# First stage of an attention and expert kernel: splits of queries and keys moved to GpSimd, a scaling moved to ScalarE, filler matmuls held in place

## The chip, the cores and the metric

The kernel runs on 1 core of one Trainium2 chip. The metric is device microseconds of one execution. Before the change three runs took 1026.7, 1026.74 and 1029.19 us, median 1026.74 us. The engines are TensorE (PE in the profile, with PEld for its weight loads), VectorE (DVE), ScalarE (ACT), GpSimd (POOL) and SyncE (SP), which issues nearly all DMAs.

## The reference

Inputs are q, k, v of shape (4, 8, 576, 64), that is 4 batches and 8 heads, a tau, and the weights of two further layers. Attention drops scores that lie more than tau below their row's maximum:

```
scores = scale * np.matmul(q, k.transpose(0, 1, 3, 2))
thresh = np.max(scores, axis=-1, keepdims=True) - tau
scores = np.where(scores >= thresh, scores, -1000000000.0)
attn = np.exp(scores - max);  attn = attn / (sum(attn) + 1e-09);  out = attn @ v
...
u = x + (x^T @ U @ V)^T ;  y = u + relu(u @ w_ch1) @ w_ch2          # channel layer
out[b, s] = p[e] * (relu(y[b, s] @ w1[e]) @ w2[e])                   # one expert of 8 per token
```

All is float32 at the borders. Operands of the large matmuls are split into a rounded high part and the rest (h and l in the names: kh, kl; w0h, w0l), so that two or three matmuls in a faster format give a product close to float32.

## The kernel before

Two heads form a pair, four pairs a batch. The first stage is the attention of batch 0 alone (attention_alone); after it each batch's attention runs interleaved with the channel layer of the batch before, then come routing and the experts.

In attention_alone a step handles one tile of 128 query rows of one head. There are 9 tiles in a pair (five groups, the last, g = 4, holds the 64 left-over rows of both heads in one tile), so 36 steps. A step's core: scores on TensorE into one of two PSUM banks (L320, L322), the row maximum on DVE (peak, L355), the limit on DVE (L359), the exponential on ScalarE (L366), threshold and row sum on DVE (mask, L370). Two steps later the result is transposed on TensorE (L423, L429) and copied out by ScalarE (L424), multiplied with v (L442 to L446), and a chain of small matmuls (L468 to L514) makes a slice of the channel layer's input.

Beside these steps runs what prepares later ones. load_pair brings a pair's keys and queries in four cuts (two of keys, two of queries) through three staging buffers called raw, which go round: each cut's DMA waits until the buffer's former user is done. Keys are rounded on ScalarE (L291) and their rest taken on GpSimd (L292); queries are scaled and rounded on ScalarE (L299), the rest on DVE (L301). A generator, conv, narrows 64-bit weights: a DMA brings a piece (cr, L203), ScalarE casts its upper part (top, L211), DVE joins the parts (w, L218), and a DMA writes the result to memory (wdram), from which load_w fetches it again (wr, L681) and splits it. For batch 0, load_w rounds the first two weight blocks on ScalarE (L688), later ones on GpSimd (L686).

Fillers are matmuls on constant data (idle, L592), issued by turn_over where a step has little TensorE work.

Each engine runs its instructions in one fixed order. A scheduler sets that order when the program is built, by its own model of time; an instruction marked with keep_in_program_order stays where it is written, and in this stage GpSimd's order is the written one. SP's queue is also in order: a DMA that waits for its buffer holds up every DMA behind it.

Of the kernel before, what the change touches and what calls it, by code (L numbers as in the profile page):

```python
# [14 lines left out]
AF = mybir.ActivationFunctionType  # L15
# [88 lines left out]
def attention_channel_moe(ctx, tc, qk, vv, tau, umat, vrep, wch, wgl, wexp, consts, out):  # L104
# [155 lines left out]
    def load_pair(b, hp, later=None):  # L260
# [9 lines left out]
            (1, 0, S), (1, S, QKW), (0, 0, 608), (0, 608, QKW))  # L270
        eng = dve if i == 0 or b > 1 else pool
        def steps():
            for n, (kq, c0, c1) in enumerate(cuts):
# [16 lines left out]
                if kq:  # L290
                    act.activation(kh[:, c], x, AF.Copy)  # L291
                    eng.tensor_tensor(out=kl[:, c], in0=x, in1=kh[:, c].bitcast(F32), op=ALU.subtract)  # L292
                elif i == 0 and c1 - c0 > 128:
                    lo, hi, xl = qs[64:128, c], qs[64:128, c].bitcast(F32), x[64:128]
# [30 lines left out]
    class Group:  # L325
# [47 lines left out]
        def norm(self):  # L373

            g = self.key[2]
            rv = self.rvs[:, g, 0:self.nh]
            if self.b >= SCALED:
                inverse(rv)
                for h in range(self.nh):
                    act.activation(self.pt[:, h], self.pt[:, h], AF.Copy, scale=rv[:, h:h + 1])  # L380
            elif g == 4:
                inverse(rv)
                sp.dma_start(out=self.rvs[:64, 4, 1:2], in_=self.rvs[64:, 4, 0:1])

# [69 lines left out]
    def chain(nm, hp, half, xT, xu, rvs):  # L454
# [20 lines left out]
        if half == 0:  # L475
            yield 0.3
            return
        if rvs is None:
            act.activation(xsd[:64, 4], tp[:64, 2], AF.Copy)
        else:  # L480
            for h in range(2):
                act.activation(xsd[:64, 4, h * 64:h * 64 + 64], tp[:64, 2, h * 64:h * 64 + 64], AF.Copy,
                               scale=rvs[:64, 4, h:h + 1])
        yield 0.3
# [75 lines left out]
    def attention_alone(b):  # L560
# [26 lines left out]
        def turn_over(n, nm):  # L587

            if n > 0:
                t = bank("tp", [128, 512], f"idle{nm}")  # L590
                for j in range(n):
                    x = pe.matmul(t, lhsT=idle[:, :128], rhs=idle, start=True, stop=True)  # L592
                    if j == 0 and nm in (0, 1, 2):
                        tc.keep_in_program_order(x)
# [3 lines left out]
        for i in range(len(seq) + 3):  # L598
# [21 lines left out]
            while pend and debt > 0:  # L620
                c = piece()
                debt -= c
                spent += c
            turn_over(int((0.8 - spent) / 0.2) + (4 if i == 0 else 0), i)
            if Q and qh == Q.nh - 1:
# [46 lines left out]
    def load_w(b, f):  # L672
# [6 lines left out]
        for i, bufs in ((0, W0), (1, W1)):  # L679
# [4 lines left out]
            eng = dve if b and (b < B - 1 or f < 8) else pool  # L684
            if b == 0 and f > 1:
                pool.tensor_copy(hi, x)  # L686
# [700 lines left out]
```

## Time and profile before

| | us |
|---|---|
| median of 3 runs | 1026.74 |
| the profiled execution | 1029.15 |
| its span, first to last instruction | 1027.4 |
| TensorE busy in the span | 993.8 (97%) |
| VectorE busy | 718.8 (70%) |
| ScalarE busy | 610.8 (59%) |
| GpSimd busy | 157.9 (15%) |

The profiled execution lies at the upper of the values that the timed runs show. A busy share is a mean over stages: the page's slices have TensorE at 8 or 9 tenths in the first five slices (to 128 us), at 9 or more after that to the end, while VectorE is at 6 to 9 tenths in the first half and 2 to 9 in the second. The first stage's last mask ends at 101.3 us, and the first matmul of the channel layer starts at 114.4 us. The mean TensorE clock over the span is 0.994.

### The profile page before, as it was taken

The page shows a single profiled execution, that of the slowest core. Times are in us where ns is not written, and L with a number is a line of the kernel's source. Part 1 is how long each engine was busy: PE and PEld are TensorE (multiplying, and loading weights), DVE is VectorE, ACT ScalarE, POOL GpSimd, SP SyncE. Part 2 cuts the span into 40 slices and gives each one's busy share as a digit, 9 for nine tenths or more (in the row PEclk, how much of TensorE's full clock was granted, in tenths as well). Part 3 has the DMA queues.
Part 4 walks back from the last instruction along what each step waited for, and adds up shares of the span by engine and source line. Part 5 has one row for each costly group of instructions (what it writes and reads, how often), then busy time and mean ns, then how long its engine had stood idle before and what let it go on. Part 6 is the DMA issues. An engine that isn't in the chain of part 4 may idle for free. (4 is left out here: it accounts for less than half of the span.)

```text
span 1027.4 us, 17797 instructions
## 1 busy us (share of the span) xinstructions
PE 993.8 (97%) x6309; PEld 831.8 (81%) x6309; DVE 718.8 (70%) x1771; ACT 610.8 (59%) x1242; POOL 157.9 (15%) x149
## 2 busy tenths in 40 slices
PE   8898899999999999999999999999999999999996
PEld 4666677778787787788888898999998798889884
DVE  7889787886778877877676564692469755566673
ACT  6787877776687777776565653432344344355562
POOL 3322145342000000000000000014400321120100
PEclk9999999999999999999999999999999999999998
DMA  7745487864323322423121110463154655566650
GB/s 216 240 126 168 144 265 241 281 204 150 114 97 92 123 80 77 125 95 89 56 68 42 42 45 28 140 212 127 39 196 151 201 178 185 174 193 198 194 184 16
DMA packets 58529, 143.72 MB, mean 140 GB/s; under 512 B 7421, under 2 KB 8573, under 8 KB 58432
## 3 DMA queue, kind: packets, MB, share of 16 engines
q1 hardware_dynamic: 55072, 132.27, 40.2%
q0 software_dynamic: 3360, 10.23, 3.0%
q8 instruction: 52, 0.85, 0.3%
q14 instruction: 45, 0.37, 0.1%
HBM read 124.65 MB, written 18.61 MB: 139 GB/s over the span
## 5 line engine op out<-in xcount | busy, mean ns | idle before, releaser
L1137 ACT ACTIVATE eh<-ew 128x512 fp32r<-128x512 f32 x160 | 94.0, 628 | 66.9 <-PE el L1253 51.8
L1138 DVE TENSOR_TENSOR el<-ew,eh 128x512 fp32r<-128x512 f32 x160 | 106.6, 692 | 37.4 <-ACT eh L1137 34.8
L370 DVE SCALAR_TENSOR_TENSOR p<-s,st,p 128x576 f32<-128x576 f32 x144 | 114.1, 814 | 18.5 <-ACT p L366 14.8
L710 PE MATMUL l<-uh,w0h 128*128 128x256 f32 (+2 forms) x352 | 126.7, 360 | 0.3 <-ACT yT L515 0.3
L366 ACT ACTIVATE p<-s,st 128x576 f32<-128x576 f32 x144 | 103.6, 739 | 34.9 <-DVE st L355 33.7
L711 PE MATMUL l<-ul,w0h 128*128 128x256 f32 (+2 forms) x352 | 122.6, 349 | 0.0
L712 PE MATMUL l<-uh,w0l 128*128 128x256 f32 (+2 forms) x352 | 122.3, 348 | 0.0
L355 DVE TENSOR_REDUCE st<-s 128x1 f32<-128x576 f32 x144 | 105.2, 749 | 16.2 <-PE s L322 15.2
L725 PE MATMUL l<-hh,w1h 128*128 128x512 f32 (+3 forms) x320 | 115.3, 360 | 0.0
L727 PE MATMUL l<-hh,w1l 128*128 128x512 f32 (+3 forms) x320 | 112.6, 352 | 0.0
L726 PE MATMUL l<-hl,w1h 128*128 128x512 f32 (+3 forms) x320 | 112.2, 351 | 0.0
L424 ACT ACTIVATE ptt<-tp 128x512 f32<-128x512 f32 (+1 forms) x192 | 88.6, 490 | 30.7 <-PE tp L423 30.5
L320 PE MATMUL s<-kh,qs 128*128 128x288 f32 x320 | 96.7, 321 | 7.1 <-DVE p L370 4.9
L689 POOL TENSOR_TENSOR w1l<-wr,w1h 128x512 fp32r<-128x512 f32 x24 | 32.4, 1359 | 457.9 <-DVE rha L995 426.2
L423 PE MATMUL tp<-cst,p 128*128 128x128 f32 x576 | 91.2, 276 | 2.6 <-ACT ptt L424 2.2
L730 DVE TENSOR_TENSOR yT<-l,yT 128x448 f32<-128x448 f32 (+2 forms) x96 | 50.0, 521 | 57.7 <-PE l L727 57.3
L322 PE MATMUL s<-kl,qs 128*128 128x288 f32 x320 | 89.6, 299 | 0.0
L380 ACT ACTIVATE p<-p,rv 128x576 f32<-128x576 f32 x108 | 78.6, 771 | 15.7 <-DVE rv L387 15.5
L423 PEld LDWEIGHTS tp<-cst,p 128*128 128x128 f32 x576 | 67.9, 140 | 19.2 <-ACT ptt L424 9.3
L320 PEld LDWEIGHTS s<-kh,qs 128*128 128x128 f32 x320 | 60.9, 190 | 17.1 <-DVE p L370 7.7
L443 PE MATMUL po<-ptt,v 128*64 128x256 f32 (+1 forms) x256 | 71.4, 416 | 2.2 <-ACT ptt L424 2.2
L442 PE MATMUL po<-ptt,v 128*64 128x256 f32 (+1 forms) x256 | 70.8, 416 | 1.3 <-ACT ptt L431 1.0
(610 smaller groups left out, 2441.1 us busy)
## 6 DMA issues: line engine op xcount, KB each, us to landing
ew<-in_wexp_dram SPq DMA_DIRECT2D x80, 512.0 KB, 4.5
wr<-wdram SPq DMA_DIRECT2D x128, 256.0 KB, 2.7
cr<-in_wch_dram SPq DMA_DIRECT2D x32, 512.0 KB, 5.4
raw<-in_qk_dram SPq DMA_DIRECT2D x30, 304.0 KB, 3.5
wdram<-w SPq DMA_DIRECT2D x32, 256.0 KB, 2.9
v<-in_vv_dram SPq DMA_DIRECT2D x16, 352.0 KB, 3.6
raw<-in_qk_dram SPq DMA_DIRECT2D x16, 320.0 KB, 3.1
raw<-in_qk_dram SPq DMA_DIRECT2D x16, 288.0 KB, 4.0
```

The lines of the kernel that those rows point to most:

```text
L320: pe.matmul(s["t"][:, h, :288], lhsT=qs[:, qc:qc + 128], rhs=kh[:, k0:k0 + 288], start=(j == 0), stop=False)
L355: dve.tensor_reduce(out=self.st[:, 0, h:h + 1], in_=self.t[h], axis=AX.XY, op=ALU.max, negate=True)
L366: act.activation(self.halves(h), self.t[h], AF.Exp, bias=self.st[:, 0, h:h + 1])
L370: dve.scalar_tensor_tensor(out=p, in0=self.t[h], scalar=self.st[:, 1, h:h + 1], in1=p, op0=ALU.is_ge, op1=ALU.mult, accum_out=self.rvs[:, ...
L423: pe.transpose(tp[:, c - c0], src[:, c * 128:c * 128 + 128], ident)
L710: pe.matmul(pm, lhsT=w1h[:, wk], rhs=uh[k], start=(k == 0), stop=False)
L711: pe.matmul(pm, lhsT=w1h[:, wk], rhs=ul[k], start=False, stop=False)
L712: pe.matmul(pm, lhsT=w1l[:, wk], rhs=uh[k], start=False, stop=(k == 3))
L725: pe.matmul(pm, lhsT=w2h[:, wd], rhs=xh, start=(f == f0), stop=False)
L726: pe.matmul(pm, lhsT=w2h[:, wd], rhs=xl, start=False, stop=False)
L727: pe.matmul(pm, lhsT=w2l[:, wd], rhs=xh, start=False, stop=(f == f0 + 3))
L1138: dve.tensor_tensor(out=lo, in0=x, in1=hi.bitcast(F32), op=ALU.subtract)
```

## The change

For pairs 1 to 4 (`own`; pair 4 is the first of batch 1) the rounding of keys moves from ScalarE to GpSimd, and the scaling, rounding and splitting of queries moves from ScalarE and DVE to three GpSimd instructions, a form used so far for two cuts of pair 0. The left-over tile of batch 0 is now normalised by ScalarE on the tile itself; before, its factors were moved to other partitions by a small DMA and applied later in two ScalarE copies. Fillers of every step but the first burst keep their place, and from step 4 on a step is filled to 1.5 units where it was 0.8. GpSimd rounds all of batch 0's weight blocks.

```
+        own = 1 <= i <= NPAIR
...
                 if kq:
-                    act.activation(kh[:, c], x, AF.Copy)
+                    if own:
+                        pool.tensor_copy(kh[:, c], x)
+                    else:
+                        act.activation(kh[:, c], x, AF.Copy)
                     eng.tensor_tensor(out=kl[:, c], in0=x, in1=kh[:, c].bitcast(F32), op=ALU.subtract)
-                elif i == 0 and c1 - c0 > 128:
+                elif own or i == 0 and c1 - c0 > 128:
                     lo, hi, xl = qs[64:128, c], qs[64:128, c].bitcast(F32), x[64:128]
                     pool.tensor_scalar(out=x, in0=x, scalar1=t8[:, 1:2], scalar2=None, op0=ALU.mult)
                     pool.tensor_copy(qs[:, c], x)
...
             elif g == 4:
                 inverse(rv)
-                sp.dma_start(out=self.rvs[:64, 4, 1:2], in_=self.rvs[64:, 4, 0:1])
+                act.activation(self.pt[:, 0], self.pt[:, 0], AF.Copy, scale=rv[:, 0:1])
...
-        if rvs is None:
-            act.activation(xsd[:64, 4], tp[:64, 2], AF.Copy)
-        else:
-            for h in range(2):
-                act.activation(xsd[:64, 4, h * 64:h * 64 + 64], tp[:64, 2, h * 64:h * 64 + 64], AF.Copy,
-                               scale=rvs[:64, 4, h:h + 1])
+        act.activation(xsd[:64, 4], tp[:64, 2], AF.Copy)
...
-                    if j == 0 and nm in (0, 1, 2):
+                    if j == 0 and nm != "a":
                         tc.keep_in_program_order(x)
...
-            turn_over(int((0.8 - spent) / 0.2) + (4 if i == 0 else 0), i)
+            turn_over(int(((1.5 if i > 3 else 0.8) - spent) / 0.2) + (4 if i == 0 else 0), i)
...
-            if b == 0 and f > 1:
+            if b == 0:
                 pool.tensor_copy(hi, x)
```

The program's order of instructions moves at three places. In the names, the first number is the pair (raw1_3: cut 3 of pair 1), in s, p, st and tp the numbers are batch, pair, group and head; the last number only tells buffers apart.

GpSimd's order from the end of pair 0's queries, before:

```order
L297 TENSOR_TENSOR qs0_97<-raw0_7_134,qs0_97 64x256
L292 TENSOR_TENSOR kl1_203<-raw1_0_204,kh1_202 128x576
L292 TENSOR_TENSOR kl1_203<-raw1_1_224,kh1_202 128x640
L236 TENSOR_TENSOR vst_65<-wv_0_342,vst_65 32x512 x2
L236 TENSOR_TENSOR vst_65<-wv_512_382,vst_65 32x64 x2
```

and now:

```order
L293 CAST kh1_202<-raw1_0_204 128x576
L296 TENSOR_TENSOR kl1_203<-raw1_0_204,kh1_202 128x576
L293 CAST kh1_202<-raw1_1_224 128x640
L296 TENSOR_TENSOR kl1_203<-raw1_1_224,kh1_202 128x640
L299 TENSOR_SCALAR raw1_2_242<-raw1_2_242,t8_63 128x608
L300 CAST qs1_201<-raw1_2_242 128x608
L301 TENSOR_TENSOR qs1_201<-raw1_2_242,qs1_201 64x608
L299 TENSOR_SCALAR raw1_3_279<-raw1_3_279,t8_63 128x608
L300 CAST qs1_201<-raw1_3_279 128x608
L301 TENSOR_TENSOR qs1_201<-raw1_3_279,qs1_201 64x608
L236 TENSOR_TENSOR vst_65<-wv_0_352,vst_65 32x512 x2
```

Two instructions on pair 1 have become ten; the last of them is the last reader of raw1_3. Pairs 2 to 4 read alike.

SP's queue has the same DMAs in the same order at that time in both programs; it stands now:

```order
L284 DMA raw1_3_279<-in_qk_dram 128x608
L308 DMA v1_200<-in_vv_dram 128x704
L203 DMA crv_512_323<-in_vrep_dram 128x256
L284 DMA raw2_0_478<-in_qk_dram 128x576
L284 DMA raw2_1_512<-in_qk_dram 128x640
L284 DMA raw2_2_541<-in_qk_dram 128x608
L203 DMA cr0_0_0_350<-in_wch_dram 128x2048
L203 DMA cr0_0_512_390<-in_wch_dram 128x2048
```

raw2_2 goes into the buffer of raw1_3, and cr0_0_0, the first piece of channel weights, is behind it. Where ScalarE turns from pair 0 to pair 1 (top is the cast of a piece, p0_1_0 the first exponential of pair 1), before:

```order
L291 ACTIVATE kh2_460<-raw2_0_462 128x576
L291 ACTIVATE kh2_460<-raw2_1_496 128x640
L366 ACTIVATE p0_0_4_322<-s0_0_4_0_324,st0_0_4_323 128x576
L449 ACTIVATE yT0_363<-po0_0_1_312 128x256
L424 ACTIVATE ptt0_0_2_365<-tp0_0_2_0_366 128x4x128
L211 ACTIVATE top1_88<-cr0_0_0_340 128x512
L424 ACTIVATE ptt0_0_2_365<-tp0_0_2_4_397 128x4x128
L424 ACTIVATE ptt0_0_2_365<-tp0_0_2_8_403 128x128
L211 ACTIVATE top0_87<-cr0_0_512_380 128x512
L366 ACTIVATE p0_1_0_349<-s0_1_0_0_352,st0_1_0_350 128x576
```

and now:

```order
L370 ACTIVATE p0_0_4_330<-s0_0_4_0_332,st0_0_4_331 128x576
L453 ACTIVATE yT0_373<-po0_0_1_320 128x256
L428 ACTIVATE ptt0_0_2_375<-tp0_0_2_0_376 128x4x128
L211 ACTIVATE top1_88<-cr0_0_0_350 128x512
L370 ACTIVATE p0_1_0_359<-s0_1_0_0_362,st0_1_0_360 128x576
L428 ACTIVATE ptt0_0_2_375<-tp0_0_2_4_407 128x4x128
L428 ACTIVATE ptt0_0_2_375<-tp0_0_2_8_413 128x128
L211 ACTIVATE top0_87<-cr0_0_512_390 128x512
L370 ACTIVATE p0_1_0_359<-s0_1_0_1_399,st0_1_0_360 128x576
L387 ACTIVATE p0_0_4_330<-p0_0_4_330,rv0_0_0_152 128x576
```

The two kh2 are gone, the cast of cr0_0_0 still stands ahead of the first exponential of pair 1, and the scaling of the left-over tile is new.

DVE's order in the third group of pair 1, before (TENSOR_REDUCE is peak, SCALAR_TENSOR_TENSOR on p is mask):

```order
L355 TENSOR_REDUCE st0_1_2_487<-s0_1_2_0_488 128x1
L355 TENSOR_REDUCE st0_1_2_487<-s0_1_2_1_514 128x1
L359 TENSOR_SCALAR st0_1_2_487<-st0_1_2_487,t8_63 128x1 x2
L386 TENSOR_SCALAR rv0_1_0_351<-rv0_1_0_351 128x4
L370 SCALAR_TENSOR_TENSOR p0_1_2_486,rv0_1_0_351<-s0_1_2_0_488,st0_1_2_487,p0_1_2_486 128x576
L370 SCALAR_TENSOR_TENSOR p0_1_2_486,rv0_1_0_351<-s0_1_2_1_514,st0_1_2_487,p0_1_2_486 128x576
```

and now:

```order
L359 TENSOR_REDUCE st0_1_2_503<-s0_1_2_0_504 128x1
L363 TENSOR_SCALAR st0_1_2_503<-st0_1_2_503,t8_63 128x1
L374 SCALAR_TENSOR_TENSOR p0_1_2_502,rv0_1_0_361<-s0_1_2_0_504,st0_1_2_503,p0_1_2_502 128x576
L476 TENSOR_TENSOR xsd0_0_1_382<-tx0_0_4_522,rv0_0_0_152 128x256
L359 TENSOR_REDUCE st0_1_2_503<-s0_1_2_1_533 128x1
L363 TENSOR_SCALAR st0_1_2_503<-st0_1_2_503,t8_63 128x1
L374 SCALAR_TENSOR_TENSOR p0_1_2_502,rv0_1_0_361<-s0_1_2_1_533,st0_1_2_503,p0_1_2_502 128x576
```

Peak and mask of one tile now follow each other, where two peaks came before two masks. On TensorE the program has 78 filler matmuls where it had 35.

## Rows read from the trace of the kernel before

**Rows 1.** Windows of three stretches: us, busy per engine (instructions), PEclk, DMA share, GB/s.

```profile
31.40:101.30 69.90, 60.47 (x433) 44.17 (x433) 61.75 (x147) 55.99 (x121) 19.15 (x15) 0.98 0.58 174
101.30:114.40 13.10, 10.81 (x78) 7.35 (x78) 10.64 (x27) 11.00 (x29) 0.00 (x0) 1.00 0.47 161
114.40:400.00 285.60, 281.90 (x1683) 218.49 (x1684) 219.26 (x483) 208.91 (x407) 60.08 (x58) 1.00 0.50 162
```

**Rows 2.** Timeline of GpSimd, 10 to 19 us: start, us, instruction, [idle before].

```profile
10.23 1.41 POOL L295 TENSOR_SCALAR raw<-raw,t 128x448 f32<-128x448 f32 x1 [8.06 <-DVE st L359]
11.71 0.56 POOL L296 CAST qs<-raw 128x448 fp32r<-128x448 f32 x1
12.36 1.13 POOL L297 TENSOR_TENSOR qs<-raw,qs 64x448 fp32r<-64x448 f32 x1
13.59 0.92 POOL L295 TENSOR_SCALAR raw<-raw,t 128x256 f32<-128x256 f32 x1
14.58 0.39 POOL L296 CAST qs<-raw 128x256 fp32r<-128x256 f32 x1
15.06 0.72 POOL L297 TENSOR_TENSOR qs<-raw,qs 64x256 fp32r<-64x256 f32 x1
15.86 2.93 POOL L292 TENSOR_TENSOR kl<-raw,kh 128x576 fp32r<-128x576 f32 x2
```

**Rows 3.** Timeline of DVE, SP and ACT, 22 to 32 us, some lines.

```profile
22.11 0.85 DVE L301 SCALAR_TENSOR_TENSOR qs<-raw,t,qs 64x608 fp32r<-64x608 f32 x1
...
22.99 0.33 SPq L283 DMA_DIRECT2D raw<-in_qk_dram  x1
23.47 0.33 SPq L203 DMA_DIRECT2D cr<-in_wch_dram  x1
...
28.86 0.79 ACT L211 ACTIVATE top<-cr 128x512 f16<-128x512 bf16 x1 [0.20 <-DMA cr<-in_wch_dram]
...
30.79 0.72 ACT L366 ACTIVATE p<-s,st 128x576 f32<-128x576 f32 x1
...
31.40 0.67 DVE L218 SCALAR_TENSOR_TENSOR w<-cr,top 128x512 int32<-128x512 int32 x1
```

**Rows 4.** View of the tile cr, 20 to 110 us: issue to landing.

```profile
DMA to landing us min/median/max: 4.3/5.3/6.0
```

**Rows 5.** Groups by line on DVE, 12 to 101 us: count | busy, mean ns.

```profile
L301 DVE SCALAR_TENSOR_TENSOR qs<-raw,t,qs 64x608 fp32r<-64x608 f32 x9 | 7.7, 851 | 0.7 <-ACT qs L299 0.4
L218 DVE SCALAR_TENSOR_TENSOR w<-cr,top 128x512 int32<-128x512 int32 x7 | 7.2, 1022 | 0.0
L386 DVE TENSOR_SCALAR rv<-rv 128x4 f32<-128x4 f32 x8 | 3.9, 493 | 0.0
```

**Rows 6.** Timeline of ACT and DVE, 46 to 52 us, lines with idle time.

```profile
46.43 0.63 ACT L688 ACTIVATE w0h<-wr 128x512 fp32r<-128x512 f32 x1 [0.84 <-DMA wr<-wdram]
...
48.05 0.82 DVE L370 SCALAR_TENSOR_TENSOR p<-s,st,p 128x576 f32<-128x576 f32 x1 [1.01 <-ACT p L366]
...
49.95 0.82 DVE L370 SCALAR_TENSOR_TENSOR p<-s,st,p 128x576 f32<-128x576 f32 x1 [0.95 <-ACT p L366]
...
51.71 0.76 DVE L355 TENSOR_REDUCE st<-s 128x1 f32<-128x576 f32 x1 [0.94 <-PE s L322]
```

**Rows 7.** Durations of two DVE lines: ns min/median/max; one instance from the timeline.

```profile
L218 DVE SCALAR_TENSOR_TENSOR w<-cr,top x7: 674/681/1999, 31.4 to 97.5; 128x512 int32<-128x512 int32 x7
...
L386 DVE TENSOR_SCALAR rv<-rv x11: 136/160/1344, 17.0 to 96.4; 128x4 f32<-128x4 f32 x8, 128x1 f32<-128x1 f32 x3
...
27.86 0.66 DVE L386 TENSOR_SCALAR rv<-rv 128x4 f32<-128x4 f32 x1
```

**Rows 8.** Timeline of DVE at 95 us: a mask right behind its tile's peak.

```profile
95.02 0.82 DVE L370 SCALAR_TENSOR_TENSOR p<-s,st,p 128x576 f32<-128x576 f32 x1 [0.56 <-ACT p L366]
```

**Rows 9.** Four fillers in the timeline; a window after TensorE had waited.

```profile
12.28 1.04 PE L592 MATMUL idle<-idle 128*128 128x512 bf16 x4
...
50.00:52.50 2.50, 2.50 (x13) 1.96 (x14) 1.56 (x4) 1.41 (x3) 1.49 (x2) 0.55 0.38 133
```

## The prediction, made before the changed kernel was run

> **What bounds the kernel now.** I read the page's slices first, then windows by stage, then the timelines of each engine in the first stage. The windows [rows 1] show two regimes. From 114.4 us TensorE is busy 281.9 of 285.6 us: the channel layer is bound by TensorE, and what comes late at its start comes late at the end, one for one. Before that, from 31.4 to 101.3 us, TensorE is busy 60.5 of 69.9, VectorE 61.8, ScalarE 56.0, GpSimd 19.2. VectorE is the fullest, and its idle time of 8.1 us is mostly waits for ScalarE or TensorE in a chain of scores, peak, exponential and mask. So the change is worth what it moves the last mask at 101.3 us and the first channel matmul at 114.4 us. GpSimd has 50 us free there, but what it takes over runs slower.
>
> **The pace of GpSimd.** The one query split that GpSimd already does gives it [rows 2]. From start to start, a cut of 448 columns takes 1.48, 0.65 and 1.23 us (scale, round, rest), one of 256 takes 0.99, 0.48 and 0.80. Per column that is 2.55, 0.89 and 2.24 ns; carried on to 608 columns: 1.89, 0.79 and 1.59, together 4.27 us a cut. Rounding the keys (576 and 640 columns) takes 0.76 and 0.82 by the same line, the two rests 2.93 as now. A pair costs 2.93 + 1.58 + 2 x 4.27 = 13.05 us. Pair 1 would run from 15.86 to 28.9. The stretch of 69.9 us holds three pairs' tiles, 23.3 us each, so GpSimd, at 13.05, isn't late for pairs 2 to 4.
>
> **SP's queue (E): +4.2.** raw2_2 goes into the buffer of raw1_3. Now its DMA leaves at 22.99, as soon as VectorE has split raw1_3 (22.11 + 0.85), and cr0_0_0 follows at 23.47 [rows 3]. With the split on GpSimd the buffer comes free at 28.9, so raw2_2 leaves at 28.95 and cr0_0_0 at 29.4. A piece lands 4.3 to 6.0 us after its issue, mostly 5.3 [rows 4]: 34.8. ScalarE's cast of it took 0.79 us with 0.20 us of waiting, and stands ahead of pair 1's first exponential (30.79) in both programs; VectorE's join w followed at 31.40. It would now start at about 35.6 instead: +4.2 us. The bounds: +3.3 with a landing of 4.3; +6.5 with one of 6.0 and 1.5 us lost by GpSimd on the way. What queues behind: on ScalarE the exponentials of pair 1, on VectorE their masks.
>
> The Trainium skill, page "Perfetto Trace Analysis", section "GPSIMD Engine Instruction", holds that GpSimd's reported spans are rough and that spacing from start to start is safer; [rows 2] agree in that the starts are 0.07 to 0.10 us further apart than the spans are long. By spans, E would be 3.5 and the total 0.7 lower; I keep to spacing, since an instruction starts no sooner than the rows show.
>
> **What VectorE is spared: -8.0.** Eight splits of queries at 851 ns leave it ([rows 5] count nine to 101.3 us; one belongs to the next pair, which keeps its form). Two of the eight lie before 31.4, where E covers them; six count: -5.1 us. The first two weight blocks are rounded by GpSimd, so ScalarE no longer stands waiting for wr (0.84 us at 46.43), after which VectorE had gaps of 1.01, 0.95 and 0.94 us [rows 6]: -2.9. What is late next there is VectorE itself.
>
> **What GpSimd takes back: +2.3.** Two VectorE forms have long versions where GpSimd is at work: the join w, 681 ns at the median but 1022 in the mean and 1999 at most, and the factors rv on 128x4, which took 0.16 at the median, 0.66 at 27.86 and 1.34 at most [rows 5, 7]. Excess: 7 x (1.022 - 0.681) + 8 x (0.493 - 0.160) = 5.0 us; 4.4 of it after 31.4 (less 0.50 at 27.86 and a little at 17.0). After the change 13 such instructions stand in the stretch, and GpSimd is busy 3 x 13.05 + 2.9 for pair 5's rests + about 4 x 1.9 for weights = 49.7 of 69.9 us, a share of 0.71. With a mean wait of 0.72 us (half of the GpSimd instruction that is met; long ones are met more often, which makes it 1.45) that is 13 x 0.71 x 0.72 = 6.7, so 2.3 more than now. Bounds: no such waits, -4.4; each of the 13 waits 1.3 us, 16.9 - 4.4 = +12.6. Now the mean excess is 0.33 us an instruction at a GpSimd share of 0.27 (19.15 of 69.9), where the same rule gives 0.20; grown with the share it would be 0.87 after the change, which is the second rival below. I take the rule's 0.51, between these and none, because both medians are the short versions.
>
> Rows show these waits beside GpSimd's subtractions and casts; none shows VectorE behind a GpSimd scaling. If that form did not hold VectorE up, the share would be 0.38 at most and the term 3.1 us lower. The Trainium skill, page "SBUF — State Buffer", section "Who interferes with whom", has a lock on a port pair that VectorE and GpSimd share, held for a whole instruction, with the other side fully blocked; by it the scaling holds VectorE up as well. That leaves the sum as it is, and speaks against the change.
>
> **Order and the rest of VectorE and ScalarE: +0.9.** Peak and mask of a tile now follow each other where two peaks stood ahead of two masks. Where that happens today, the mask waits 0.56 us for its exponential [rows 8]. Four more such places, 2.2, and 0.5 for one with the new xsd between them, less 1.0 for what today's order loses there (my estimate, two waits of this kind): +1.7. The second peak of pair 1 stands behind the late w: +0.7. ScalarE loses the rounding of four pairs and gains four scalings of about 0.77 us (a ScalarE instruction of 576 columns took 0.72 [rows 3]); its shorter queue ends some of VectorE's other waits sooner: -1.5 (0 to -4).
>
> **Fillers and clock: +1.0.** 43 more fillers at 0.26 us (four took 1.04 [rows 9]) are 11 us of work for TensorE, whose idle time in the stretch is 9.4 us [rows 1]. Placed in the waits they cost nothing, placed ahead of scores they push a chain. Against that they keep the clock up: after TensorE waited at about 48 us the granted clock was 0.55 in 50.0 to 52.5 us [rows 9], the lower level. While it waits for E a fall of this kind is likely again. Bounds 0 and +4.
>
> **Tail: +0.2.** The left-over tile is scaled on ScalarE ahead of its transposes (0.77), with one copy and one small DMA fewer: -0.5 to +0.8.
>
> **Sum.** 4.2 - 5.1 - 2.9 + 2.3 + 0.9 + 1.0 + 0.2 = +0.6 us, on the profiled execution's 1029.15 (span 1027.4, the rest lies around it). That execution was 2.4 us above the median of 1026.74, so against the median I predict 1027.3.
>
> **Rivals.** *Faster: the queue isn't in the way.* If GpSimd ends raw1_3 sooner, or the piece lands while ScalarE is busy anyway, E is gone: 0.6 - 4.2 = -3.6; with waits on GpSimd at the level of now, another -2.3, about 1021 to 1023.5; I give 1022. For it: VectorE and ScalarE are the fullest engines of the stretch and both are relieved. Against it: 23.47 follows 22.96 directly, and the 0.20 us of waiting at 28.86 show ScalarE already on that DMA. Chance 0.34.
>
> *Slower: each blocked VectorE instruction waits for a whole GpSimd instruction.* The place is w and rv, the price at least 1.0 us for 13 instructions rather than the mean of 0.51: +6.3, at 1033.6. It decides from a mean wait of 0.75 us on. For it: 1999 and 1344 ns at most [rows 7]; against it: the medians are the short versions. Chance 0.17. The Trainium skill's lock on the port pair (page "SBUF — State Buffer", section "Who interferes with whom") is this mechanism at its strongest, when GpSimd issues back to back.
>
> *Slower: the piece lands at its upper bound,* and TensorE, having waited, restarts at the lower clock with fillers ahead of scores: E 6.5 (+2.3) and fillers at about +2.5 (+1.5), so 1031. For it: the window at 0.55; against it: the held fillers run in that very wait. Chance 0.11.
>
> That the change doesn't do what it says can be left out: the order shows each instruction at its new engine.
>
> **How the numbers follow.** 0.3% is 3.1 us, about what a measurement of this kernel can tell from no change: 1023.7 to 1029.8 is "same". The forecast, 1027.3 with its own range of 1024 to 1030, has a chance of 0.38. The faster rival's 0.34 makes the chance of faster, the two slower ones' 0.28 that of slower. The range takes in the faster rival down to 1018 (waits on GpSimd at the low bound) and the slower ones up to 1035; beyond lie the sums of several bounds of one sign, which I leave to 2 in 10.
>
> **What would show it.** E: SP's issue of cr0_0_0 at 29 to 30 us instead of 23.5, top with a wait of several us on cr, w at about 35.6. If cr0_0_0 leaves before 26 us, E is wrong and the result is nearer 1022. Spared work: no L301 split on VectorE for pairs 1 to 4, no wait for wr in the window of 46 to 52 us. Waits on GpSimd: the mean of w and of rv on 128x4; w above 1.5 us and rv above 0.8 would bear out the slower rival, w near 0.7 the faster one. GpSimd: scale, round and rest starting 1.89, 0.79 and 1.59 us apart. Order: waits of masks on the exponential of their own tile of about 0.5 us. Clock: PEclk in 30 to 40 us. The whole: the last mask at about 101.7 and the first channel matmul at 115.0. If these two move by other than the total does, the later stages changed as well, and the one-for-one carry is wrong.

## The result, and the profile after

The changed kernel took 1037.19 us (median of 4 runs) against 1027.24 for the kernel before beside it: ratio 1.0087, 95% interval 1.007 to 1.0104. It is about 10 us slower where I had forecast no change, and outside my range. The profiled execution took 1036.35 us, span 1034.6, so 7.2 us more than that of before; the latter was 1.9 us above the median of 1027.24 and the changed one 0.8 below its own, which is the rest of the 10.

The windows of the changed kernel answer to [rows 1]: from the first join w to the last mask, from there to the first channel matmul, then the channel layer (us, then busy time of TensorE, its weight loads, VectorE, ScalarE, GpSimd with instructions, granted clock, DMA share, GB/s). The fourth is the stretch in which I expected the clock to fall.

```profile
33.97:107.35 73.38, 68.00 (x463) 49.83 (x469) 57.60 (x140) 50.54 (x108) 49.42 (x42) 0.98 0.52 160
107.35:122.26 14.91, 11.95 (x89) 8.36 (x88) 12.71 (x33) 13.01 (x33) 0.69 (x1) 1.00 0.52 177
122.26:400.00 277.74, 273.45 (x1623) 211.42 (x1623) 212.54 (x470) 203.36 (x394) 60.31 (x58) 1.00 0.50 162
30.00:40.00 10.00, 7.96 (x42) 6.25 (x42) 8.36 (x25) 6.72 (x14) 8.80 (x9) 0.83 0.90 271
```

The last mask ends at 107.35 (before 101.3), the first channel matmul starts at 122.26 (114.4): +6.1 and +7.8, and the span grew by 7.2. So the loss lies in the first stage and is carried on nearly one for one. VectorE did 4.2 us less work in the stretch, with no split of queries left in it, and stood idle for 15.8 us of it where it had been 8.2. TensorE was busy 68.0 us, 7.5 more. What VectorE waited for is in the view of waits, first of the kernel before (29.2 to 101.3 us), then of the changed one (31.7 to 107.4): engine, tile, line, releaser, us in total, times, longest. Lines shift in the changed kernel: scores end at L326 (L322 before), peak is L359 (L355), mask L374 (L370).

```profile
DVE p L370 <- ACT p L366: 3.0, 5, 1.0
DVE st L355 <- PE s L322: 2.6, 5, 0.9
```

```profile
DVE st L359 <- PE s L326: 8.3, 10, 1.9
DVE p L374 <- ACT p L370: 5.2, 8, 1.2
DVE w L218 <- ACT top L211: 0.9, 1, 0.9
```

The wait for scores grew from 2.6 to 8.3 us: VectorE now waits most for what TensorE has still to do ahead of the scores.

GpSimd ran as calculated. Its timeline (start, us, instruction) has the three instructions of a cut 1.86, 0.78 and 1.59 us apart, against 1.89, 0.79 and 1.59 worked out from [rows 2]:

```profile
19.70 1.80 POOL L299 TENSOR_SCALAR raw<-raw,t 128x608 f32<-128x608 f32 x1
21.56 0.69 POOL L300 CAST qs<-raw 128x608 fp32r<-128x608 f32 x1
22.34 1.49 POOL L301 TENSOR_TENSOR qs<-raw,qs 64x608 fp32r<-64x608 f32 x1
23.93 1.80 POOL L299 TENSOR_SCALAR raw<-raw,t 128x608 f32<-128x608 f32 x1
25.80 0.69 POOL L300 CAST qs<-raw 128x608 fp32r<-128x608 f32 x1
26.57 1.49 POOL L301 TENSOR_TENSOR qs<-raw,qs 64x608 fp32r<-64x608 f32 x1
```

Beside it, in the timeline of VectorE, SP and ScalarE, stands what the split did to others:

```profile
22.42 1.59 DVE L218 SCALAR_TENSOR_TENSOR wu<-cru,top 128x160 int32<-128x160 int32 x1
24.05 0.74 DVE L229 COPY u_sb<-wu 128x160 f32<-128x160 f32 x1
27.24 1.37 DVE L218 SCALAR_TENSOR_TENSOR wv<-crv,top 128x512 int32<-128x512 int32 x1 [0.80 <-ACT top L211]
28.47 4.78 SPq L203 DMA_DIRECT2D cr<-in_wch_dram  x3
33.10 0.78 ACT L211 ACTIVATE top<-cr 128x512 f16<-128x512 bf16 x1 [1.00 <-DMA cr<-in_wch_dram]
33.97 1.15 DVE L218 SCALAR_TENSOR_TENSOR w<-cr,top 128x512 int32<-128x512 int32 x1 [0.89 <-ACT top L211]
```

cr0_0_0 leaves SP at 28.47 where it left at 23.47 [rows 3]. wu, u_sb and wv (the joins of the channel layer's U and V, and a copy of the first) took 0.31, 0.24 and 0.68 us before (rows below): 2.5 us lost to GpSimd ahead of the first w, which my sum, beginning at 31.4 us, did not hold. These are the groups by line, the first fence of before, the second of after:

```profile
L218 DVE SCALAR_TENSOR_TENSOR wv<-crv,top 128x512 int32<-128x512 int32 x1 | 0.7, 680 | 0.0
L218 DVE SCALAR_TENSOR_TENSOR wu<-cru,top 128x160 int32<-128x160 int32 x1 | 0.3, 314 | 0.0
L229 DVE COPY u_sb<-wu 128x160 f32<-128x160 f32 x1 | 0.2, 236 | 0.0
```

```profile
L218 DVE SCALAR_TENSOR_TENSOR w<-cr,top 128x512 int32<-128x512 int32 x7 | 7.8, 1110 | 0.9 <-ACT top L211 0.9
L390 DVE TENSOR_SCALAR rv<-rv 128x4 f32<-128x4 f32 x8 | 2.7, 342 | 0.1
```

### The profile page after: what moved, and what is told of

Same layout as the page of the kernel before. It is cut to its first block, busy times and chain, and to the rows that moved or that the text cites. A ratio compares the mean times of both kernels' runs of the same rounds, so it can differ in the third digit from the quotient of the medians.

```text
span 1034.6 us, 17862 instructions
## 1 busy us (share of the span) xinstructions
PE 1003.0 (97%) x6343; PEld 838.5 (81%) x6352; DVE 716.1 (69%) x1763; ACT 602.5 (58%) x1222; POOL 198.0 (19%) x185
## 5 line engine op out<-in xcount | busy, mean ns | idle before, releaser
L370 ACT ACTIVATE p<-s,st 128x576 f32<-128x576 f32 x144 | 103.8, 738 | 50.8 <-DVE st L359 49.5
L374 DVE SCALAR_TENSOR_TENSOR p<-s,st,p 128x576 f32<-128x576 f32 x144 | 114.1, 814 | 20.1 <-ACT p L370 16.7
L359 DVE TENSOR_REDUCE st<-s 128x1 f32<-128x576 f32 x144 | 105.6, 750 | 23.6 <-PE s L326 22.7
L324 PE MATMUL s<-kh,qs 128*128 128x288 f32 x320 | 99.0, 329 | 5.5 <-DVE p L374 2.9
L326 PE MATMUL s<-kl,qs 128*128 128x288 f32 x320 | 89.7, 299 | 0.0
L384 ACT ACTIVATE p<-p,rv 128x576 f32<-128x576 f32 x108 | 78.6, 771 | 15.5 <-DVE rv L391 15.4
L446 PE MATMUL po<-ptt,v 128*64 128x256 f32 (+1 forms) x256 | 70.6, 414 | 2.3 <-ACT ptt L435 1.0
L709 PEld LDWEIGHTS l<-uh,w0h 128*128 128x128 f32 x352 | 66.4, 189 | 7.1 <-ACT yT L514 1.0
```

What stands on the lines that cost most here:

```text
L324: pe.matmul(s["t"][:, h, :288], lhsT=qs[:, qc:qc + 128], rhs=kh[:, k0:k0 + 288], start=(j == 0), stop=False)
L359: dve.tensor_reduce(out=self.st[:, 0, h:h + 1], in_=self.t[h], axis=AX.XY, op=ALU.max, negate=True)
L370: act.activation(self.halves(h), self.t[h], AF.Exp, bias=self.st[:, 0, h:h + 1])
L374: dve.scalar_tensor_tensor(out=p, in0=self.t[h], scalar=self.st[:, 1, h:h + 1], in1=p, op0=ALU.is_ge, op1=ALU.mult, accum_out=self.rvs[:, ...
L709: pe.matmul(pm, lhsT=w1h[:, wk], rhs=uh[k], start=(k == 0), stop=False)
```

## The experiments

Every ratio is to the kernel before on the same chip; "last mask" and "first matmul" (of the channel layer) are us in the run's profiled execution. The expectations name theories by letters: A is the split on GpSimd, B the fillers, C the scaling on ScalarE, Q the loop through SP's queue, L the waits of VectorE on GpSimd; E is the late cr0_0_0 of the prediction.

| run | ratio, 95% interval | last mask | first matmul |
|---|---|---|---|
| before | 1 | 101.3 | 114.4 |
| changed | 1.0087 (1.0070 to 1.0104) | 107.4 | 122.3 |
| u_split | 1.0065 (1.0040 to 1.0090) | 104.9 | 119.8 |
| u_fill | 1.0041 (1.0025 to 1.0056) | 100.4 | 119.4 |
| u_norm | 1.0115 (1.0078 to 1.0152) | 106.6 | 122.1 |
| u_w | 1.0174 (1.0143 to 1.0204) | 117.9 | 132.8 |
| u_splitfill | 1.0027 (1.0009 to 1.0045) | 100.6 | 113.6 |
| a_fill | 1.0115 (1.0090 to 1.0140) | 108.2 | 123.7 |
| u_lvl | 1.0027 (1.0014 to 1.0040) | 101.0 | 114.7 |
| u_fill_own2 | 1.0013 (0.9991 to 1.0036) | 96.7 | 116.4 |
| own23 | 1.0066 (1.0047 to 1.0086) | 108.6 | 121.6 |
| own13 | 1.0094 (1.0072 to 1.0115) | 108.7 | 121.7 |
| thin | 1.0073 (1.0049 to 1.0096) | 105.0 | 120.1 |
| a_split | 1.0072 (1.0051 to 1.0094) | 108.5 | 122.1 |
| poolq2 | 1.0073 (1.0044 to 1.0101) | 96.9 | 118.5 |
| ownk | 1.0072 (1.0045 to 1.0099) | 107.3 | 120.3 |
| kl5dve | 1.0029 (1.0010 to 1.0047) | 95.8 | 116.0 |
| kl5dve_conv | 1.0020 (1.0006 to 1.0035) | 98.9 | 114.7 |

No version beats the kernel before. The two columns of times are one execution each, up to 3.1 us from the run's median, and from the first channel matmul to the end of the span the runs take 912.3 to 920.2 us (913.0 before). So a ratio that differs by a few thousandths need not come from the first stage.

**One part undone at a time.**

u_split: `own = False`.

> The changed kernel with queries and keys of pairs 1 to 4 split as before the change (ScalarE and VectorE); scaling of the left-over tile, fillers and weight rounding stay changed. Theory A (the split on GpSimd is what costs: VectorE blocked early on wu, wv and u_sb, 2.5 us; the late cr0_0_0, 2.4; scores whose operands and copies come late): most of the 10 us goes, 1027 to 1030. Theory B (held and more numerous fillers put scores late on TensorE, the 8.3 us in which VectorE waits for scores): stays at 1034 to 1037, less only the early 2 to 3 us. Theory C (scaling on ScalarE ahead of exponentials): stays at 1035 or above.

1.0065, an interval that overlaps the changed kernel's. Theory A falls in its plain form: with the fillers in place, the split is not the bulk.

u_fill:

```
-                    if j == 0 and nm != "a":
+                    if j == 0 and nm in (0, 1, 2):
...
-            turn_over(int(((1.5 if i > 3 else 0.8) - spent) / 0.2) + (4 if i == 0 else 0), i)
+            turn_over(int((0.8 - spent) / 0.2) + (4 if i == 0 else 0), i)
```

> The changed kernel with the fillers as before the change (a step filled to 0.8, only those of the first three steps held); all else stays changed. Theory A: no help, 1035 to 1038. Theory B: VectorE's waits for scores fall from 8.3 us to the 2.6 of the kernel before, so 5 to 7 us go, 1030 to 1032. Theory C: 1035 to 1038.

1.0041: 0.0046 of 1027 less than the changed kernel, 4.7 us, and the last mask 7 us earlier; of these the first channel matmul keeps 2.9, since the stretch behind the mask is 19.0 us. The time is what theory B had expected. But with the fillers gone term E comes into view whole. The timeline of ScalarE and VectorE:

```profile
34.40 0.77 ACT L211 ACTIVATE top<-cr 128x512 f16<-128x512 bf16 x1 [4.84 <-DMA cr<-in_wch_dram]
35.26 0.69 DVE L218 SCALAR_TENSOR_TENSOR w<-cr,top 128x512 int32<-128x512 int32 x1 [4.84 <-ACT top L211]
```

u_norm: the small DMA and the two scaled ScalarE copies of xsd are back, the scaling of the tile is out.

> The changed kernel with the left-over tile's factors moved by the small DMA and applied in two ScalarE copies, as before the change. Theory A and theory B: within 1.5 us of the changed kernel, 1036 to 1038. Theory C: the masks' waits for their exponential, 5.2 us, fall to about the 3.0 of before, and the time by 2 to 4 us, 1033 to 1035.

1.0115, not lower (the intervals overlap): theory C falls. ScalarE's scaling costs nothing that shows.

u_w: `if b == 0 and f > 1:` again.

> The changed kernel with the first two weight blocks rounded on ScalarE, as before the change. My prediction had -2.9 us for this part of the change, so undoing it should cost 2 to 3 us, 1039 to 1040, if ScalarE's wait for the block stands there again. If VectorE was waiting for scores at that time anyway: no difference, 1036 to 1038.

1.0174: undoing it costs 8.9 us, three times what I had expected. ScalarE's view of waits (28 to 120 us) says why: the blocks come late, and now ScalarE stands before them.

```profile
ACT w1h L687 <- DMA wr<-wdram: 8.0, 2, 5.7
```

**Fillers.**

u_splitfill: `own = False` and the fillers of u_fill.

> The changed kernel with both the split on GpSimd and the fillers undone: what is left of the change is the scaling of the left-over tile on ScalarE and the rounding of the first two weight blocks on GpSimd. Theory AB (split and fillers together are the whole loss, the rest gains by ScalarE no longer waiting for wr): 1022 to 1025. If the two parts that are left bring nothing while the pieces come in time: 1026 to 1028. If the scaling costs: above 1028.

1.0027, at the edge of what can be told from no change: the scaling and the rounding alone bring nothing. It lies just above 1028, where I would have blamed the scaling; u_norm doesn't bear that out, and what the 2.8 us are stays open. The 2.9 us of [rows 6] that I had booked as a gain aren't there.

a_fill: the kernel before with only

```
-                    if j == 0 and nm in (0, 1, 2):
+                    if j == 0 and nm != "a":
...
-            turn_over(int((0.8 - spent) / 0.2) + (4 if i == 0 else 0), i)
+            turn_over(int(((1.5 if i > 3 else 0.8) - spent) / 0.2) + (4 if i == 0 else 0), i)
```

> The kernel before with only the fillers changed (held, filled to 1.5: 78 instead of 35). Theory B (43 fillers at 0.26 us are 11 us on a TensorE that has 9.4 us idle in the first stage): 1031 to 1034. If they cost only together with the split on GpSimd, because VectorE sets the pace without it: 1026 to 1028.

1.0115, 11.8 us, and more than theory B had expected: about the whole of the 11 us that 43 fillers last. VectorE's waits in it (29.2 to 108 us), and two of the fillers in TensorE's timeline:

```profile
DVE st L355 <- PE s L322: 10.4, 11, 2.9
DVE p L370 <- ACT p L366: 4.1, 6, 1.1
```

```profile
32.76 1.02 PE L592 MATMUL idle<-idle 128*128 128x512 bf16 x4 [1.14 <-ACT ptt L424]
...
58.27 1.02 PE L592 MATMUL idle<-idle 128*128 128x512 bf16 x4 [1.02 <-ACT ptt L424]
```

The waits for scores are four times those of before, although no split was moved. A filler not only lasts: it is written into a bank of the transposes (`bank("tp", ...)`), and here it stood 1.14 and 1.02 us for ScalarE to empty one, with all of TensorE's queue behind it.

u_lvl: as the changed kernel, with `(0.8 - spent)` again but every filler still held.

> The changed kernel filled to 0.8 again (35 fillers), but each still held at its step. If the number of fillers costs: like the run with the fillers undone, 1030 to 1033. If holding them costs (scores kept behind them): like the changed kernel, 1035 to 1038.

1.0027: it is their number, not the holding. This run says something on the split too, which it has whole. The late piece is there, and GpSimd waits 17.3 us for weight blocks, yet the last mask (101.0) and the first channel matmul (114.7) come as before the change; what is left of its loss lies behind them. In its view of ScalarE's waits (28 to 118 us):

```profile
ACT top L211 <- DMA cr<-in_wch_dram: 5.4, 1, 5.4
```

So these waits have no fixed price: it depends on the order of work around them.

thin: 64 columns in a filler instead of 512, from step 4 on.

```
+                    m = 64 if nm != "a" and nm > 3 else 512
-                    x = pe.matmul(t, lhsT=idle[:, :128], rhs=idle, start=True, stop=True)
+                    x = pe.matmul(t[:, :m], lhsT=idle[:, :128], rhs=idle[:, :m], start=True, stop=True)
```

> The changed kernel with as many fillers at the same steps, but those of step 4 and later 64 columns wide where they were 512. Theory B (the fillers cost by TensorE's time): like the run with the fillers undone, 4 to 6 us less than the changed kernel, ratio 1.003 to 1.005. If they cost by their place in the order, because scores and transposes stand behind them: like the changed kernel, ratio 1.008 to 1.010.

1.0073, between the two theories, with an interval that overlaps the changed kernel's; VectorE's wait for scores is 7.3 us in the same stretch. Short fillers are nearly as bad as long ones by these runs, so their time on TensorE seems not to be the whole of it (by their spans it is 4.3 us from 31 to 108 us, against 10.0 in the changed kernel); that the bank is the rest fits these rows, but no run took the bank away.

**The split and the queues.**

a_split: the kernel before with only the split (`own`) moved.

> The kernel before with only the split of pairs 1 to 4 moved to GpSimd; ScalarE still rounds the first two weight blocks. Theory Q: the late pieces make ScalarE wait for wr, as the 8.0 us in the run that undid only the weight rounding, and GpSimd holds pair 5's buffers at the end: ratio 1.006 to 1.012. If VectorE's spared 6 us prevail: ratio 0.994 to 0.998.

1.0072, as theory Q had it. ScalarE waits 5.6 us for cr and 3.2 for wr, not 8.0 as in u_w. I had not named a third wait: this version still has the small DMA of the left-over tile's factors, which now leaves SP behind four cuts, at 72.87, and ScalarE waits for it (xsd is the copy that applies the factors):

```profile
75.65 0.31 ACT L486 ACTIVATE xsd<-tx,rv 64x64 f32<-64x64 f32 x1 [3.13 <-DMA rv<-rv]
```

The changed kernel has no such DMA, so these 7.4 us aren't the price of the split within it.

u_fill_own2: u_fill with `own = 2 <= i <= NPAIR`.

> The changed kernel with the fillers undone and with pair 1 split as before the change; GpSimd splits pairs 2 to 4 only. Term E (the piece cr0_0_0 is late because raw2_2 waits for pair 1's last cut) is then gone: ScalarE's wait of 4.8 us at the first cast goes, and weight blocks come earlier, so that GpSimd's wait for w1h and with it ScalarE's 3.9 us for raw at 107 us shrink too: 1023 to 1027. If waits of VectorE on GpSimd, or the later pairs' buffers, are what is left of the loss: 1029 to 1032.

1.0013 against u_fill's 1.0041: without pair 1's split, E's wait is gone, worth 0.0028 or 2.9 us (the intervals overlap; the first channel matmul is 3.0 us earlier). The last mask is 4.6 us earlier than before the change: the time spared on VectorE is real here. It is lost behind that mask, where the stretch to the first matmul is 19.8 us instead of 13.1:

```profile
107.88 0.80 ACT L303 ACTIVATE qs<-raw,t 128x608 fp32r<-128x608 f32 x1 [4.18 <-DMA raw<-in_qk_dram]
```

```profile
100.97 0.61 POOL L685 CAST w1h<-wr 128x512 fp32r<-128x512 f32 x1 [7.34 <-DMA wr<-wdram]
```

GpSimd stands before a late weight block; behind it is the rest of pair 5's keys, which holds the buffer that ScalarE's cut is to come into. And TensorE stands behind ScalarE. Its timeline and a window (granted clock third from the end):

```profile
109.83 0.90 PE L472 MATMUL tx<-cst,yT 128*128 128x128 f32 x3 [4.66 <-ACT yT L453]
```

```profile
110.00:112.00 2.00, 2.00 (x15) 1.51 (x19) 1.66 (x6) 0.68 (x2) 0.00 (x0) 0.50 0.88 261
```

After that wait TensorE works at the lower of its two clock levels, 0.50 from 110 to 114 us, so the wait costs more than its own length. The same is seen in u_fill, kl5dve and poolq2 below: where TensorE waits 4.3 to 6.0 us behind the last mask, the stretch is 19.0 to 21.6 us; in the kernel before, the changed one, u_lvl and kl5dve_conv its longest wait there is 1.8 us, and the stretch 13.1 to 15.8.

own23 and own13: u_fill with `own = 2 <= i < NPAIR` and `own = 1 <= i < NPAIR`.

> The changed kernel with the fillers undone and GpSimd splitting pairs 2 and 3 only (pairs 1 and 4 as before the change). Theory Q (what is left of the loss is SP's queue: a cut of pair 1 and one of pair 4 that wait for GpSimd hold up the pieces and weight blocks behind them; VectorE's spared time is real): the last mask stays near the 96.7 us of the run that splits pairs 2 to 4, plus about 2 us for pair 4's two splits on VectorE, and the stretch to the first channel matmul falls from 19.8 to about 13 us: 3 to 4 us faster than the kernel before, ratio 0.996 to 0.997. Theory L (waits of VectorE on GpSimd's port eat the gain): same time as before or slower, ratio 1.000 to 1.003.

> As the run with pairs 2 and 3 only, but GpSimd splits pair 1 too. Theory Q, term E: 3 to 5 us slower than with pairs 2 and 3, by a wait of 4 to 5 us of ScalarE for cr0_0_0; ratio to the kernel before about 1.000. If E is made good later in the stage: the same as with pairs 2 and 3.

Theory Q's forecast for own23 fell: 1.0066, not 0.997. Its part E is half borne out, the wait but not its price. own13 is 0.0028 slower (the intervals overlap), and ScalarE's wait for cr, which own23 lacks, is there (ScalarE's timeline):

```profile
33.41 0.78 ACT L211 ACTIVATE top<-cr 128x512 f16<-128x512 bf16 x1 [4.72 <-DMA cr<-in_wch_dram]
```

But the last mask and the first channel matmul are only 0.1 us later than in own23, so E was made good within the stage: a later wait for pair 4's queries is 6.5 us in own13 where own23 has 9.4. The difference in the profiled executions arose behind the first channel matmul (916.8 us to the end of the span against 912.8). What happened in own23 is in the timelines of SP, GpSimd and ScalarE:

```profile
60.67 13.14 SPq L284 DMA_DIRECT2D raw<-in_qk_dram  x4
73.91 0.38 SPq L242 DMA_DIRECT2D wdram<-w  x1
74.34 0.42 SPq L203 DMA_DIRECT2D cr<-in_wch_dram  x1
77.45 0.33 SPq L680 DMA_DIRECT2D wr<-wdram  x1
...
84.54 1.82 SPq L284 DMA_DIRECT2D raw<-in_qk_dram  x2
```

```profile
81.20 0.62 POOL L685 CAST w1h<-wr 128x512 fp32r<-128x512 f32 x1 [7.74 <-DMA wr<-wdram]
81.90 1.26 POOL L688 TENSOR_TENSOR w1l<-wr,w1h 128x512 fp32r<-128x512 f32 x1
83.12 2.89 POOL L296 TENSOR_TENSOR kl<-raw,kh 128x576 fp32r<-128x576 f32 x2
```

```profile
87.34 0.80 ACT L303 ACTIVATE qs<-raw,t 128x608 fp32r<-128x608 f32 x1 [9.44 <-DMA raw<-in_qk_dram]
```

Read downwards, it is a loop through two ordered queues. Four cuts wait in SP's queue for buffers that GpSimd frees; the narrowed weights (wdram, then wr) stand behind them; GpSimd waits for that block; the rest of pair 4's keys stands behind it and holds the buffers; so the last cut leaves only at 84.54; and ScalarE, with its exponentials, waits 9.4 us for it. TensorE waits 11.1 us for ScalarE's copies, and when it works again its granted clock is 0.50 from 90 to 92 us and 1.00 from 94.

own23_wrfree and before_wrfree take the late block away:

```
+            src = qk[i][:, 1, :512] if b == 0 and f < 2 else wdram[f * 128:f * 128 + 128, i * 512:i * 512 + 512]
-            sp.dma_start(out=x, in_=wdram[f * 128:f * 128 + 128, i * 512:i * 512 + 512])
+            sp.dma_start(out=x, in_=src)
```

> As the run in which GpSimd splits pairs 2 and 3 (ratio 1.0066), but the loads of the first two weight blocks of batch 0 read an input tensor that is ready, and not the narrowed weights, so the channel layer of batch 0 computes with other numbers there. Theory Q (loop of SP's and GpSimd's queues through the weight block): GpSimd's waits of 7.7 and 15.4 us for wr and ScalarE's 9.4 us for raw go; last mask at 97 to 100 us, ratio 0.995 to 0.999. Theory L (GpSimd's speed or shared port): 1.005 to 1.008 as with the late block.

> The kernel before with the same edit: the loads of the first two weight blocks of batch 0 read an input tensor that is ready, so that batch's channel layer computes with other numbers there. Control: the kernel before loses 0.8 us on ScalarE's wait for wr and up to 2.9 us in the gaps behind it, so 0.997 to 1.000 by either theory; if it gains as much as the other run does, that run says nothing on the split.

With other numbers in batch 0 the later stages had more to do in both (1.0515 and 1.0523), so only the first stage can be compared. The wait of 9.4 us is gone, and the last mask ends at 103.6 us, 5.0 earlier than in own23; in the control it is at 101.7, as before. So the loop is shown in own23, and its price there is about 5 us, with what the clock adds to it. Theory Q had expected more, a last mask at 97 to 100. GpSimd's second wait did not go, as it is for the block after those two:

```profile
97.09 0.61 POOL L686 CAST w1h<-wr 128x512 fp32r<-128x512 f32 x1 [16.73 <-DMA wr<-wdram]
```

That 103.6 is still 1.9 us later than the control says that the loop is not all; the granted clock, 0.93 from 31 to 103 us against 1.00 in the control, is one candidate.

poolq2: u_fill_own2 with the DMAs of the split pairs issued by GpSimd (`pool.dma_start`, each one cut ahead).

> The changed kernel with the fillers undone, GpSimd splitting pairs 2 to 4 (ratio 1.0013 so), and the DMAs of those pairs' cuts issued by GpSimd itself, so that they no longer stand in SP's queue ahead of pieces and weight blocks. Theory Q: pieces leave as early as in the kernel before (the seventh at about 61 us, not 73), no wait for raw of 4 us at 107 us; ratio 0.994 to 0.998, less what issuing twelve DMAs costs GpSimd. Theory L: unchanged or worse, 1.001 to 1.005.

The pieces left as early as before (the seventh at 59.1 us), and the last mask stayed at 96.9, but the stretch behind it is 21.6 us: 1.0073. ScalarE waits 5.5 us for a cut of pair 5, which leaves SP only once GpSimd, after 8.7 us before a weight block, has taken the rest of that pair's first keys:

```profile
103.06 0.78 POOL L697 CAST w1h<-wr 128x512 fp32r<-128x512 f32 x1 [8.65 <-DMA wr<-wdram]
```

```profile
106.91 0.33 SPq L296 DMA_DIRECT2D raw<-in_qk_dram  x1
```

Taking the cuts of pairs 2 to 4 out of SP's queue does not open the loop: pair 5's cuts still stand in it, and the ring of three buffers is shared. Of the 11.3 us by which its profiled span is longer than that of before, only 4.1 stand at the first channel matmul; the rest came later, and why is open.

ownk: u_fill with keys alone rounded on GpSimd.

> The changed kernel with the fillers undone and GpSimd only rounding the keys of pairs 1 to 4; queries are split by ScalarE and VectorE as before. Theory Q: the query cuts free their buffers early, cr0_0_0 leaves before 26 us, no long wait of ScalarE for raw; VectorE is spared nothing, ScalarE 1.3 us a pair: ratio 0.997 to 1.001. Theory L: waits of w and rv as before the change, so also 0.998 to 1.002; above 1.003 neither holds.

1.0072, which neither theory had. E is gone (cr0_0_0 leaves at 24.6), no long wait for raw, yet VectorE waits 7.1 us for scores. Why stays open: each edit also makes the scheduler write another order for TensorE and ScalarE.

kl5dve, kl5dve_conv: u_fill_own2 with the rest of pair 5's keys on VectorE; the second also with `debt += 0.25` for 0.2 in the pace of pieces.

> The changed kernel with the fillers undone, GpSimd splitting pairs 2 to 4, and the rest of pair 5's keys on VectorE instead of GpSimd. Theory Q (loop through GpSimd and SP): the last mask stays near 97 us, ScalarE's wait of 4.2 us for raw at the end of the stage goes, and the stretch from the last mask to the first channel matmul falls from 19.8 to 13 to 15 us: ratio 0.994 to 0.997, faster than both kernels. Theory L (GpSimd's speed, shared port): 1.000 to 1.003 as before.

> As the run with the rest of pair 5's keys on VectorE, with pieces narrowed at 0.25 a step instead of 0.2, so that each weight block stands earlier in SP's and GpSimd's order. Theory Q: GpSimd's waits for wr (6.6 and 7.3 us) shrink further; about 1 us of VectorE and ScalarE work moves from the later stage into the first: ratio 0.993 to 0.998. If the later stage gets nothing back for it: 0.997 to 1.001.

Theory Q's forecasts of 0.994 to 0.997 and 0.993 to 0.998 fell. The stretch behind the last mask did not shorten in kl5dve (20.2 us): without pair 5's keys on GpSimd another wait takes their place. The same ScalarE instruction still waits 4.04 us, now for the cut that leaves SP at 97.11: it stands behind a weight block (wr) that is fetched only once the write issued at 92.86 has landed, and lands 4.8 us after its issue.

```profile
92.86 0.38 SPq L242 DMA_DIRECT2D wdram<-w  x1
93.30 0.42 SPq L203 DMA_DIRECT2D cr<-in_wch_dram  x1
93.82 0.42 SPq L308 DMA_DIRECT2D v<-in_vv_dram  x1
96.70 0.33 SPq L680 DMA_DIRECT2D wr<-wdram  x1
97.11 0.38 SPq L284 DMA_DIRECT2D raw<-in_qk_dram  x1
```

With earlier pieces it fell to 15.8 us, but the last mask came 3.1 us later. Both stay just above the kernel before.

## Why the prediction was wrong, point by point

**Fillers and clock, +1.0.** This step failed most. I had worked out 11 us of fillers for 9.4 us of idle TensorE, and then wrote that placed in the waits they cost nothing. Measured: 4.7 us within the change (u_fill), 11.8 alone (a_fill). TensorE's idle time was made of waits of up to 1.9 us, for ScalarE's copies and for a bank that a mask frees; what ends such a wait then stands behind the filler in an ordered queue. My upper bound of +4 took them as a nuisance, not as work on the path. The clock did fall where I expected it: 0.83 from 30 to 40 us, 0.98 over the stretch as before [rows 1]. In u_fill, without the added fillers, it was 0.66 there; what the fillers saved by that was less than they cost.

**What VectorE is spared, -8.0.** The splits left as counted; the time did not come back. I had taken the fullest engine for the bound, with 8.2 us idle, when the chain through TensorE and ScalarE was as long: VectorE's idle time went to 15.8 us. Only with the fillers and pair 1's split undone did the last mask come more than 1 us earlier, by 4.6 us in u_fill_own2. The second half of this term, 2.9 us for ScalarE's wait for wr, was the wrong thing to count: in u_splitfill it brings nothing, but in the changed kernel the rounding on GpSimd avoids 8.9 us, because the blocks had become late through SP's queue.

**SP's queue, +4.2.** The mechanism is borne out, the size in part: cr0_0_0 left at 28.47 (I had 29.4), and with the fillers undone ScalarE waited 4.84 us. In the changed kernel itself only 1.00 us of that wait is seen, as ScalarE was late already, and the first join w stands at 33.97, 2.6 us later than before, where I had 35.6. Net it is worth 2.9 us between u_fill and u_fill_own2, 0.1 at the first channel matmul between own23 and own13, and nothing at that place in u_lvl. What I missed is that it doesn't happen once. Each pair's cuts stand in SP's queue ahead of a piece or block, and from the first block on GpSimd waits for one itself. That loop cost about 5 us in own23, where it was taken apart; waits of the same kind stand at the end of the stage in u_fill, u_fill_own2 and poolq2, where their price was not isolated, and in u_lvl they cost nothing by the first channel matmul.

**What GpSimd takes back, +2.3.** From 12 to 107 us, w and rv lose 7 x (1.110 - 0.681) + 8 x (0.342 - 0.160) = 4.5 us, less than the 5.0 of before: the term is -0.5. But wu, u_sb and wv lost 2.5 us ahead of the stretch, where I hadn't looked. The second rival, whole waits on w and rv, is out. One figure of my working here was wrong, though the sum does not use it: without the scalings GpSimd would be busy 38.4 of 69.9 us, a share of 0.55 and not 0.38, which makes the term 1.5 us lower and not 3.1.

**Order, +0.9.** The masks' waits for their exponential grew by 2.2 us (3.0 to 5.2), near the 1.7 I had for peak and mask side by side. The relief of 1.5 us that I set against it isn't visible.

**Tail, +0.2.** The stretch from the last mask to the first matmul grew by 1.8 us. The scaling isn't the cause (u_norm: 15.5 us against 14.9).

**Rivals.** The faster one fell, since E was there. Of the slower ones the last, late cr with fillers ahead of scores, had the two right mechanisms; its 1031 has too low a price for the fillers. The other, at 1033.6, is nearer in number, but by the waits on w and rv that are out.

**One for one.** Held for this pair of executions: +7.8 us at the first channel matmul, +7.2 in the span. It does not hold for every run: poolq2's profiled execution lost another 7.2 us behind that matmul.

What stays open: the parts do not add up. Split and fillers alone cost 7.4 and 11.8 us, the whole change 9 to 10. With an order that is rewritten for each edit, I can say what two mechanisms cost where they were isolated, not how the whole divides. Nearest to an account of it: with the fillers undone 1.0087 falls to 1.0041, and with pair 1's split undone as well to 1.0013, which can't be told from no change.

## What to carry to other kernels

Filling a queue that runs in order is free only where nothing behind the filler is about to be released: compare the fillers' time with the idle time that they are to fill, and price the excess in full. Before work moves to a slower engine, follow each buffer it frees to the queue that waits for it, and on to what that engine itself waits for; where that closes a loop, the freed time can come back as a wait at the next turn. The engine with the highest busy share isn't the bound as long as it idles in waits for a chain that is as long as its own work.

## What the runs showed of the hardware that I had not expected

VectorE's wu started at 22.42, as GpSimd's TENSOR_TENSOR began at 22.34, and ended 0.18 us after that one's end at 23.83, 1.59 us instead of 0.31. Beside a scaling the wait was shorter: u_sb, at 24.05, took 0.74 instead of 0.24, though the TENSOR_SCALAR that began at 23.93 has a span of 1.80. A second such place:

```profile
43.22 1.80 POOL L299 TENSOR_SCALAR raw<-raw,t 128x608 f32<-128x608 f32 x1
```

```profile
43.54 0.47 DVE L390 TENSOR_SCALAR rv<-rv 128x4 f32<-128x4 f32 x1
```

rv took 0.47 instead of 0.16 and was done 1.0 us before that scaling's span ended. So a GpSimd scaling does delay VectorE, which no row had shown ahead of the change, but by 0.3 to 0.5 us in these two. The rule of the Trainium skill that I had cited ("SBUF — State Buffer", section "Who interferes with whom"), a lock for the whole instruction, agrees with the first case; in the other two the measured wait is shorter, as far as GpSimd's spans can be trusted.
